# A delta-rule attention and a cosine feed-forward layer on one core: the order of 2143 tasks written anew

## The chip, the cores and the metric

The kernel runs on one core of a Trainium2 chip. The metric is device time in microseconds, from the first to the last instruction of the core and what lies around it; lower is better. The engines are TensorE (PE in the profile, with its weight loads as PEld), VectorE (DVE), ScalarE (ACT), GpSimd (POOL) and SyncE (SP), which here only issues DMAs.

## The reference

The first half is a recurrence over 768 steps with a 48 x 48 state for each of 4 x 8 heads, the second half a feed-forward layer with the activation h cos(h) on the 3072 x 384 result.

```python
k_n = k / (np.linalg.norm(k, axis=-1, keepdims=True) + 1e-06)
for t in range(S):                                   # S = 768, B = 4, H = 8, D = 48
    kt, vt, bt = (k_n[:, :, t], v[:, :, t], beta[:, :, t, None])
    y[:, :, t] = np.einsum('bhd,bhde->bhe', q[:, :, t], state)
    v_old = np.einsum('bhde,bhd->bhe', state, kt)
    state = state + bt[:, :, :, None] * np.einsum('bhd,bhe->bhde', kt, vt - v_old)
x = y.transpose(0, 2, 1, 3).reshape(3072, 384)
h = x @ w_in                                         # 384 x 2048
out = (h * np.cos(h)) @ w_out                        # 2048 x 384
```

## The kernel before

**Tasks.** The sequence is cut into 24 units of 32 steps; two units make a pair. The kernel first writes down 2143 tasks, each with a key, a Python function that issues its instructions on one engine, the tasks that it depends on, and the buffers that it makes and uses. Then `Order.run` (line 195) calls them one after the other in the order of `LINE` (line 79), a list of 2143 numbers, each the place of a task in the list of keys: 497 is `eye(7)`, 449 is `put(6)`, 739 is `hidden(0,0)`. At the end each engine's instructions are pinned to one another, so `LINE` fixes the order of every engine's queue and of SyncE's. A task that must wait holds up all that stands behind it on its engine. The costs and due times given to `add` are not used by `run`.

**Sides.** `OTHER` (line 49) holds the keys of tasks that go to their second engine: `x_sum` goes to GpSimd, or to VectorE if named in `OTHER`; `left` and `in_sums` go to VectorE, or to GpSimd if named; `fold` and `unfold` go to VectorE, or to ScalarE if named.

**Attention.** For each unit n, `k(n)`, `q(n)` and `v(n)` load keys, queries and values (from unit 8 on, `blocks` loads keys and queries once more, for a transpose on VectorE). `square`, `sum`, `norms` and `scale` form the norms of the keys; `turn` and `turn_out` transpose; `gram` multiplies keys with keys and queries, and `gram_keys` and `gram_queries` copy the result out of PSUM. A unit's triangular system is inverted next. In units 0 to 3 this is done on the spot: `fold`, `fold_in` and `fold_off` split the matrix, `rows` (TensorE) spreads its rows and `eliminate` works them off, on VectorE for groups 0 and 1 (units 0 and 1) and on GpSimd for group 2 (units 2 and 3, through `rows_copy` on ScalarE); then come `unfold`, `solve_half`, `half_out`, `between` and `between_out`. From unit 4 on a pair m is inverted on GpSimd: `gram_put` (L760) writes both matrices to DRAM, `gram_get(m)` (L769) reads them back into `gb`, `eye(m)` (L776, ScalarE) fills `z` with the identity, `inv(m,0)` to `inv(m,6)` (L791, L798) invert, `put(m)` (L802) writes `z` to DRAM, and `get(2m)` and `get(2m+1)` (L811) fetch it as the blocks that `solve` multiplies with. There is one `gb` and one `z`, so `eye(m+1)` waits until `put(m)`'s DMA has read `z`. Then follow `solve` (L891), `solve_out` (L901), `update` and `update_out` (the state, L914, L922), `within` (L931), `within_out`, `features` and `features_out` (the unit's columns of x). `state(n)` (L828) needs `update_out(n-1)`: the units are a chain.

**Feed-forward.** The weights come as 64-bit words and are narrowed on the chip: `weights(t)`, `split(t)`, `shift(t)` and `add(t)` on SyncE, ScalarE, VectorE and GpSimd. Pairs 0 and 1 compute h plainly (`hidden`, L971, 24 matrix products each), the other ten with twenty block products instead of 24: sums of parts of x (`x_sum`, L1064) and of w_in (`in_sums`, L1111) are multiplied in `layer(p,i)` (L1149) and put together in `layer_out` (L1161, L1163 on ScalarE, L1166 on VectorE). The activation is `turns` (L1012, ScalarE), `rest` (L1019, VectorE), `cos` (L1028, ScalarE) and `gate` (L1031, VectorE). The last product is plain in pair 0 (L1172) and Strassen's seven products from pair 1 on: `out(p,step,part)` (L1229), with `left` (L1245) forming sums of the activations, `right` (L1258) sums of w_out, `collect` (L1281, one in seven on ScalarE, L1268) adding the products up, and `store` (L1293) writing the output. PSUM holds three banks for h and two halves of one for the output.

The few lines that decide the order:

```python
line = [keys[int(i)] for i in self.LINE.split()]
for key in line:
    emit, deps, makes, uses = self.tasks[key]
    assert deps <= done, key
    emit()
```

Of the kernel before, what the change touches and what calls it, by code (L numbers as in the profile page):

```python
# [46 lines left out]
class Order:  # L47

    OTHER = {
        ('weigh', 0, 0), ('fold', 0), ('unfold', 0), ('weigh', 0, 1), ('fold', 1), ('unfold', 1),  # L50
        ('fold', 2), ('fold', 3), ('unfold', 2), ('unfold', 3), ('in_sums', 6), ('in_sums', 8),
        ('in_sums', 14), ('in_sums', 15), ('x_sum', 2, 'd'), ('x_sum', 2, 'n'), ('x_sum', 2, 'm'),
        ('x_sum', 2, 'e'), ('x_sum', 2, 'k'), ('x_sum', 2, 'g'), ('x_sum', 2, 'i'),
        ('x_sum', 2, 'l'), ('x_sum', 2, 'f'), ('x_sum', 2, 'h'), ('x_sum', 2, 'b0'),
        ('left', 2, 1, 0), ('left', 2, 2, 0), ('left', 2, 3, 1), ('x_sum', 3, 'd'),
        ('x_sum', 3, 'n'), ('x_sum', 3, 'm'), ('x_sum', 3, 'e'), ('x_sum', 3, 'k'),
        ('x_sum', 3, 'g'), ('x_sum', 3, 'i'), ('x_sum', 3, 'l'), ('x_sum', 3, 'h'),
        ('x_sum', 3, 'b0'), ('left', 3, 1, 0), ('left', 3, 4, 0), ('x_sum', 4, 'd'),
        ('x_sum', 4, 'n'), ('x_sum', 4, 'm'), ('x_sum', 4, 'e'), ('x_sum', 4, 'k'),
        ('x_sum', 4, 'l'), ('x_sum', 4, 'f'), ('x_sum', 4, 'h'), ('x_sum', 4, 'b0'),  # L60
        ('left', 4, 4, 0), ('left', 4, 3, 0), ('left', 4, 3, 1), ('x_sum', 5, 'd'),
        ('x_sum', 5, 'n'), ('x_sum', 5, 'k'), ('x_sum', 5, 'g'), ('x_sum', 5, 'b0'),
        ('left', 5, 1, 1), ('left', 5, 4, 0), ('left', 5, 3, 0), ('left', 5, 3, 1),
        ('x_sum', 6, 'd'), ('x_sum', 6, 'n'), ('x_sum', 6, 'k'), ('x_sum', 6, 'g'),
        ('left', 6, 1, 0), ('left', 6, 2, 0), ('left', 6, 2, 1), ('left', 6, 4, 1),
        ('left', 6, 3, 0), ('x_sum', 7, 'd'), ('x_sum', 7, 'n'), ('x_sum', 7, 'm'),
        ('x_sum', 7, 'l'), ('x_sum', 7, 'h'), ('x_sum', 7, 'b0'), ('left', 7, 1, 0),
        ('left', 7, 3, 0), ('x_sum', 8, 'd'), ('x_sum', 8, 'n'), ('x_sum', 8, 'm'),
        ('x_sum', 8, 'g'), ('x_sum', 8, 'l'), ('x_sum', 8, 'h'), ('x_sum', 8, 'b0'),
        ('x_sum', 9, 'd'), ('x_sum', 9, 'f'), ('left', 9, 1, 0), ('left', 9, 2, 0),  # L70
        ('left', 9, 1, 1), ('left', 9, 4, 0), ('left', 9, 4, 1), ('left', 9, 3, 0),
        ('left', 9, 3, 1), ('x_sum', 10, 'd'), ('x_sum', 10, 'n'), ('x_sum', 10, 'm'),
        ('x_sum', 10, 'g'), ('x_sum', 10, 'i'), ('x_sum', 10, 'l'), ('x_sum', 10, 'b0'),
        ('left', 10, 1, 0), ('left', 10, 2, 1), ('left', 10, 3, 0), ('x_sum', 11, 'd'),
        ('x_sum', 11, 'n'), ('x_sum', 11, 'f'), ('x_sum', 11, 'h'), ('left', 11, 1, 0),
        ('left', 11, 4, 0), ('left', 11, 4, 1), ('left', 11, 3, 0), ('left', 11, 3, 1),
# [1729 lines left out]
```

## Time and profile before

| | |
|---|---|
| time, median of 3 runs | 652.16 us (648.83 to 653.66) |
| span of the profiled execution | 654.2 us |
| TensorE busy | 619.1 us, 95%, 12306 matrix instructions |
| VectorE busy | 505.7 us, 77%, 948 instructions |
| ScalarE busy | 265.5 us, 41%, 469 instructions |
| GpSimd busy | 451.1 us, 69%, 788 instructions |
| chain that ended last | PE 72%, POOL 8%, DVE 7%, DMA 6%, issue 3% |

Busy times are of one execution under the profiler, whose span is its own time. A line of instructions gives the engine, the line of the code, the operation, what it wrote and read, and in brackets the idle time of the engine before it with what ended it. SPq is SyncE's queue, where the time is that of issuing DMAs.

### The profile page before, as it was taken

How to read it: one execution, taken by the hardware profiler on the slowest of the kernel's cores; microseconds unless marked ns; L12 is line 12 of the kernel's file. 1: busy time of each engine (PE TensorE's matmuls, PEld its weight loads, DVE VectorE, ACT ScalarE, POOL GpSimd, SP SyncE). 2: the span in 40 equal slices, each digit the busy share in tenths (PEclk: the TensorE clock that was granted, in tenths of full speed). 3: DMA queues.
4: the chain of work that ended last, by engine and by line, in shares of the span. 5: the costliest groups of instructions: out<-in, count | busy, mean ns of one | idle time of the engine just before them, and what ended most of it. 6: DMA issues, size and time to landing. Idle time of an engine off the chain costs nothing.

```text
span 654.2 us, 28227 instructions
## 1 busy us (share of the span) xinstructions
PE 619.1 (95%) x12306; PEld 579.8 (89%) x12306; DVE 505.7 (77%) x948; ACT 265.5 (41%) x469; POOL 451.1 (69%) x788
## 2 busy tenths in 40 slices
PE   5879799999999999998899999999999999999996
PEld 4778798976989999898799999999999999999996
DVE  7789798878999979776787877777777668667681
ACT  3545575731224523611542533622534523435340
POOL 3348989978988888686788986697787584143103
PEclk9979899999999999999799999999999999999999
DMA  7882573555444554434415434423400403000001
GB/s 157 192 217 72 130 217 82 118 107 75 90 68 67 115 73 71 95 67 81 77 29 93 67 62 77 90 40 62 85 7 13 105 4 60 13 2 25 2 13 36
DMA packets 202623, 49.99 MB, mean 76 GB/s; under 512 B 194244, under 2 KB 197460, under 8 KB 202500
## 3 DMA queue, kind: packets, MB, share of 16 engines
q1 hardware_dynamic: 201236, 47.81, 38.0%
q8 instruction: 96, 1.57, 1.0%
q10 hardware_dynamic: 1088, 0.20, 0.2%
q0 software_dynamic: 176, 0.18, 0.1%
q14 instruction: 27, 0.22, 0.1%
HBM read 38.19 MB, written 9.96 MB: 74 GB/s over the span
## 4 chain that ended last, share of the span: by engine, by line
PE 72%; POOL 8%; DVE 7%; DMA 6%; issue 3%; SPq 2%; ACT 2%; DVEq 0%; ACTq 0%; POOLq 0%
PE p_out L1229 23%; PE p_h L1149 23%; PE p_h L971 7%; PE p_out L1172 3%; DMA out_dram<-o 3%; PE p_kq L828 3%; PE p_u L891 2%; PE p_s L914 2%; POOL z L798 2%; POOL part L791 2%; PE p_kq L931 2%; PE p_g L619 2%; DVE turns L1019 1%; DMA qp<-in_q_dram 1%; PE p_z L950 1%
## 5 line engine op out<-in xcount | busy, mean ns | idle before, releaser
L791 POOL TENSOR_TENSOR part<-z,gb 128x126 f32<-128x126 f32 (+22 forms) x310 | 139.4, 450 | 56.2 <-DMA gb<-g_dr 15.7
L798 POOL TENSOR_TENSOR z<-z,part 128x126 f32<-128x126 f32 (+22 forms) x310 | 140.5, 453 | 24.4
L1229 PE MATMUL p_out<-w_out,g_ffn 128*128 128x192 f32 x672 | 122.5, 332 | 1.5 <-DVE o L1281 1.5
L1229 PEld LDWEIGHTS p_out<-w_out,g_ffn 128*128 128x128 f32 x672 | 109.0, 192 | 3.0 <-issue 1.1
L1028 ACT ACTIVATE turns<-turns,halfpi 128x512 f32<-128x512 f32 x96 | 68.7, 721 | 75.4 <-DVE turns L1019 74.8
L1229 PE MATMUL p_out<-w_sum,g_ffn 128*128 128x192 f32 x496 | 89.6, 329 | 1.8 <-DVE o L1281 1.8
L1245 POOL TENSOR_TENSOR g_ffn<-g_ffn 128x512 f32<-128x512 f32 x34 | 46.6, 1380 | 62.1 <-DVE g_ffn L1031 31.8
L1149 PE MATMUL p_h<-x_sum,w_in 128*128 128x128 f32 x640 | 84.8, 279 | 0.7 <-DVE g_ffn L1166 0.7
L1229 PEld LDWEIGHTS p_out<-w_sum,g_ffn 128*128 128x128 f32 x496 | 79.6, 191 | 2.9 <-DVE o L1281 2.2
L1149 PEld LDWEIGHTS p_h<-x_sum,w_in 128*128 128x128 f32 x640 | 78.7, 193 | 2.7 <-DVE g_ffn L1166 1.5
L1012 ACT ACTIVATE turns<-g_ffn,quarter_turn 128x512 int32<-128x512 f32 x70 | 50.0, 720 | 48.4 <-DVE g_ffn L1166 32.6
L1166 DVE TENSOR_TENSOR g_ffn<-g_ffn,p_h 128x512 f32<-128x512 f32 x80 | 54.2, 680 | 14.7 <-PE p_h L1149 12.1
L1019 DVE SCALAR_TENSOR_TENSOR turns<-g_ffn,turns 128x512 f32<-128x512 f32 x70 | 57.6, 831 | 8.6 <-ACT turns L1012 8.5
L1031 DVE TENSOR_TENSOR g_ffn<-turns,g_ffn 128x512 f32<-128x512 f32 x70 | 52.6, 758 | 12.7 <-ACT turns L1028 12.7
L1281 DVE SCALAR_TENSOR_TENSOR o<-p_out,o 128x192 f32<-128x192 f32 x74 | 25.1, 352 | 39.8 <-PE p_out L1229 29.7
L1149 PE MATMUL p_h<-x_sum,in_sum 128*128 128x128 f32 x400 | 54.2, 280 | 1.1 <-ACT p_h L1161 0.6
L971 PE MATMUL p_h<-x_ffn,w_in 128*128 128x128 f32 x384 | 50.4, 293 | 1.5 <-ACT row_copies L712 1.5
L1149 PEld LDWEIGHTS p_h<-x_sum,in_sum 128*128 128x128 f32 x400 | 49.2, 192 | 2.3 <-ACT p_h L1161 0.8
L971 PEld LDWEIGHTS p_h<-x_ffn,w_in 128*128 128x128 f32 x384 | 47.9, 206 | 2.5 <-ACT row_copies L712 1.6
L535 POOL TENSOR_TENSOR knrm<-ksum,halves 128x16 f32<-128x16 f32 (+1 forms) x14 | 37.0, 2646 | 15.7 <-DVE ksum L523 9.0
L1245 DVE TENSOR_TENSOR g_ffn<-g_ffn 128x512 f32<-128x512 f32 x54 | 42.5, 789 | 0.9 <-POOL part L791 0.3
L1149 PE MATMUL p_h<-x_ffn,w_in 128*128 128x128 f32 x320 | 42.8, 277 | 0.0
(144 smaller groups left out, 1041.5 us busy)
## 6 DMA issues: line engine op xcount, KB each, us to landing
gb<-g_dr SPq DMA_DIRECT2D x20, 256.0 KB
vp<-in_v_dram SPq DMA_DIRECT2D x96, 48.0 KB
in_sum<-in_moe_w_out_dram SPq DMA_DIRECT2D x12, 384.0 KB
out_dram<-o SPq DMA_DIRECT2D x23, 192.0 KB
in_sum<-in_moe_w_in_dram SPq DMA_DIRECT2D x8, 512.0 KB
kp<-in_k_dram SPq DMA_DIRECT2D x128, 24.0 KB
z_dr<-z SPq DMA_DIRECT2D x10, 256.0 KB
zt<-z_dr SPq DMA_DIRECT2D x80, 32.0 KB
```

The source lines that it names most:

```text
L535: nc.gpsimd.tensor_tensor(out=scales[m][2][:, part], in0=sums[m, part.start][:, 0:n], in1=halves[:, 0:n], op=ALU.pow,)
L791: nc.gpsimd.tensor_tensor(out=part, in0=z[:, 0:rows, j, None].to_broadcast(shape), in1=a[:, j, None, j + 1 :].to_broadcast(shape), op=ALU. ...
L798: nc.gpsimd.tensor_tensor(out=behind, in0=behind, in1=part, op=ALU.subtract)
L971: nc.tensor.matmul(p_h[:, i], w_in[:, t, (4 * k + i) * 128 : (4 * k + i + 1) * 128], xts[p][:, t, unit * 128 : (unit + 1) * 128], start=(i ...
L1012: nc.scalar.activation(turns[p, f], hidden_of(p, f), AF.Identity, bias=quarter_turn, scale=TURN)
L1019: nc.vector.scalar_tensor_tensor(out=r, in0=hidden_of(p, f), scalar=TURN, in1=t, op0=ALU.mult, op1=ALU.subtract,)
L1028: nc.scalar.activation(r, r, AF.Sin, bias=halfpi, scale=2.0 * math.pi)
L1031: nc.vector.tensor_tensor(out=place(p, f), in0=step_of(rests.pop((p, f)), f), in1=step_of(hidden_of(p, f), f), op=ALU.mult,)
L1149: nc.tensor.matmul(p_h[:, e], in_block(*w)[:, e], x_of(p, b), start=new and e == 0, stop=True, skip_group_check=True,)
L1166: nc.vector.tensor_tensor(out=part_of(p, to), in0=part_of(p, one), in1=part_of(p, two), op=op)
L1229: nc.tensor.matmul(p_o, left(p, part, a)[:, e % 4], right(e, b), start=(e == 0), stop=(e == FT // 2 - 1), skip_group_check=True,)
L1245: either(("left", p, x, s), nc.vector, nc.gpsimd).tensor_tensor(out=left(p, s, to), in0=left(p, s, one), in1=left(p, s, two), op=op)
```

## The change

The list `LINE` is replaced by another permutation of the same 2143 numbers, and `OTHER` by another set. Nothing else is touched: the tasks, their instructions, buffers and dependencies are the same. 31 `x_sum` go from VectorE to GpSimd and 19 the other way; 16 `left` go from GpSimd to VectorE and 15 the other way; four `in_sums` go from GpSimd to VectorE and one the other way; three `fold` and one `unfold` go from ScalarE to VectorE.

```diff
     OTHER = {
-        ('weigh', 0, 0), ('fold', 0), ('unfold', 0), ('weigh', 0, 1), ('fold', 1), ('unfold', 1),
-        ('fold', 2), ('fold', 3), ('unfold', 2), ('unfold', 3), ('in_sums', 6), ('in_sums', 8),
-        ('in_sums', 14), ('in_sums', 15), ('x_sum', 2, 'd'), ('x_sum', 2, 'n'), ('x_sum', 2, 'm'),
...
+        ('weigh', 0, 0), ('unfold', 0), ('weigh', 0, 1), ('fold', 1), ('unfold', 1),
+        ('unfold', 2), ('in_sums', 18), ('x_sum', 2, 'n'), ('x_sum', 2, 'm'), ('x_sum', 2, 'k'),
+        ('x_sum', 2, 'g'), ('x_sum', 2, 'i'), ('x_sum', 2, 'l'), ('x_sum', 2, 'f'),
...
     LINE = """
-2031 0 1 9 10 2 3 15 16 17 11 54 55 18 56 57 21 4 60 22 23 19 58 61 62 6 24 25 26 27 28 30 34 63 64
-29 93 92 101 65 66 32 102 31 2032 2035 2036 73 95 33 35 36 37 14 123 39 20 40 96 97 2037 2039 2038
...
+9 92 0 15 16 1 2 2031 3 2035 123 54 2039 21 93 17 4 60 55 11 6 22 7 95 18 10 56 57 19 96 23 5 61 62
+24 26 27 28 63 64 29 2032 2043 126 25 124 14 30 2033 2047 32 34 97 101 39 2034 65 31 127 2036 2040
...
```

In the names of the tasks, the stretches of the two orders that come up below (`-` before, `+` after), each a part of one queue:

```
ScalarE, around eye(7)
- layer_out(4,30) turns(4,(0,1,0)) eye(7) cos(4,(0,1,0)) turns(4,(1,0,0)) cos(4,(1,0,0))
  layer_out(5,5) layer_out(5,1) turns(4,(1,1,0)) square(8,0) turns(4,(1,0,1))
+ layer_out(4,30) features_out(11) turns(4,(0,1,1)) cos(4,(0,1,1)) turns(4,(1,0,0)) cos(4,(0,1,0))
  turns(4,(0,0,1)) cos(4,(1,0,0)) layer_out(5,5) layer_out(5,1) square(8,0) eye(7) turns(4,(1,0,1))
SyncE, around put(6)
- k(19) gram_put(14) gram_put(15) put(6) gram_get(7) get(12)
+ k(19) gram_put(14) gram_put(15) put(6) blocks(17,1) gram_get(7) get(12)
TensorE, ahead of solve(12)
- out(3,5,1) layer(5,15) out(3,6,0) solve(12)
+ layer(5,15) out(3,5,0) out(3,5,1) layer(5,4) layer(5,10) layer(5,1) out(3,6,0) solve(12)
SyncE, start
- weights(0) q(2) k(2) weights(1) v(0) k(3) weights(2) q(3) weights(3) q(4) weights(4)
+ k(2) weights(0) weights(1) k(3) weights(2) q(2) weights(3) q(3) v(0) weights(4) q(4)
TensorE, start
- gram(0) gram(1) rows(0,0) rows(0,2) turn(2) rows(0,1) rows(1,2) rows(0,3) state(0) turn(3)
+ gram(0) gram(1) rows(0,0) rows(0,1) rows(0,2) turn(2) state(0) rows(0,3) turn(3)
ScalarE, start
- square(0,0) square(0,1) turn_out(0) turn_out(1) fold(0) fold_off(0) fold(1) turn_out(2) split(0)
+ square(0,0) square(0,1) turn_out(0) square(1,0) turn_out(1) fold_off(0) split(0) square(1,1) fold(1)
VectorE, start
- scale(0,1) spread(0,0) spread(0,1) gram_keys(0) gram_queries(0) fold_in(0) gram_keys(1)
  gram_queries(1) begin_rows(0) fold_in(1) eliminate(0,0) eliminate(0,1) eliminate(0,2) eliminate(0,3)
  right(0) sum(1,0) shift(1) shift(0) shift(2) between_out(0)
+ scale(0,1) spread(0,0) sum(1,0) gram_keys(0) fold(0) fold_in(0) gram_keys(1) gram_queries(1)
  begin_rows(0) gram_queries(0) shift(0) eliminate(0,0) sum(1,1) eliminate(0,1) fold_in(1)
  eliminate(0,2) eliminate(0,3) right(0) scale(1,0) shift(3) scale(1,1) shift(2) between_out(0)
TensorE, from rows(1,3) on
- rows(1,3) gram(3) hidden(0,0) rows(2,0) rows(2,1) rows(2,2) solve_half(1) between(1) hidden(0,2)
  solve(1) rows(2,3) update(1) rows(2,4) within(1)
+ rows(1,3) rows(2,0) rows(2,1) hidden(0,0) solve_half(1) rows(2,2) between(1) rows(2,3) rows(2,4)
  solve(1) hidden(0,2) update(1) within(1)
SyncE, end
- store(10,1) store_left(11) store(10,0) store(11,1) store_right(11)
+ store(10,0) store(10,1) store_left(11) store(11,1) store_right(11)
```

More of the change, by code (lines that the diff above doesn't have):

```diff
@@ L49 @@
     OTHER = {
-        ('weigh', 0, 0), ('fold', 0), ('unfold', 0), ('weigh', 0, 1), ('fold', 1), ('unfold', 1),
-        ('fold', 2), ('fold', 3), ('unfold', 2), ('unfold', 3), ('in_sums', 6), ('in_sums', 8),
-        ('in_sums', 14), ('in_sums', 15), ('x_sum', 2, 'd'), ('x_sum', 2, 'n'), ('x_sum', 2, 'm'),
-        ('x_sum', 2, 'e'), ('x_sum', 2, 'k'), ('x_sum', 2, 'g'), ('x_sum', 2, 'i'),
-        ('x_sum', 2, 'l'), ('x_sum', 2, 'f'), ('x_sum', 2, 'h'), ('x_sum', 2, 'b0'),
-        ('left', 2, 1, 0), ('left', 2, 2, 0), ('left', 2, 3, 1), ('x_sum', 3, 'd'),
@@ L56 @@
[L56 to L73, printed above, removed]
@@ L74 @@
-        ('left', 10, 1, 0), ('left', 10, 2, 1), ('left', 10, 3, 0), ('x_sum', 11, 'd'),
-        ('x_sum', 11, 'n'), ('x_sum', 11, 'f'), ('x_sum', 11, 'h'), ('left', 11, 1, 0),
-        ('left', 11, 4, 0), ('left', 11, 4, 1), ('left', 11, 3, 0), ('left', 11, 3, 1),
+        ('weigh', 0, 0), ('unfold', 0), ('weigh', 0, 1), ('fold', 1), ('unfold', 1),
+        ('unfold', 2), ('in_sums', 18), ('x_sum', 2, 'n'), ('x_sum', 2, 'm'), ('x_sum', 2, 'k'),
+        ('x_sum', 2, 'g'), ('x_sum', 2, 'i'), ('x_sum', 2, 'l'), ('x_sum', 2, 'f'),
@@ new lines @@
+        ('left', 2, 1, 0), ('left', 2, 3, 1), ('x_sum', 3, 'i'), ('x_sum', 3, 'l'),
+        ('x_sum', 3, 'f'), ('x_sum', 3, 'h'), ('x_sum', 3, 'b0'), ('left', 3, 4, 0),
+        ('left', 3, 3, 1), ('x_sum', 4, 'd'), ('x_sum', 4, 'n'), ('x_sum', 4, 'm'),
+        ('x_sum', 4, 'e'), ('x_sum', 4, 'h'), ('left', 4, 1, 0), ('left', 4, 3, 1),
+        ('x_sum', 5, 'd'), ('x_sum', 5, 'n'), ('x_sum', 5, 'm'), ('x_sum', 5, 'e'),
+        ('x_sum', 5, 'i'), ('x_sum', 5, 'h'), ('left', 5, 4, 0), ('left', 5, 4, 1),
@@ new lines @@
+        ('left', 5, 3, 0), ('left', 5, 3, 1), ('x_sum', 6, 'd'), ('x_sum', 6, 'n'),
+        ('x_sum', 6, 'm'), ('x_sum', 6, 'k'), ('x_sum', 6, 'g'), ('x_sum', 6, 'i'),
+        ('x_sum', 6, 'l'), ('x_sum', 6, 'b0'), ('left', 6, 2, 0), ('left', 6, 2, 1),
+        ('left', 6, 4, 0), ('left', 6, 4, 1), ('x_sum', 7, 'd'), ('x_sum', 7, 'm'),
+        ('x_sum', 7, 'g'), ('x_sum', 7, 'l'), ('x_sum', 7, 'h'), ('x_sum', 7, 'b0'),
+        ('left', 7, 1, 1), ('left', 7, 3, 0), ('left', 7, 3, 1), ('x_sum', 8, 'f'),
@@ new lines @@
+        ('x_sum', 8, 'h'), ('left', 8, 1, 0), ('left', 8, 3, 0), ('left', 8, 3, 1),
+        ('x_sum', 9, 'n'), ('x_sum', 9, 'e'), ('x_sum', 9, 'i'), ('x_sum', 9, 'f'),
+        ('left', 9, 1, 0), ('left', 9, 4, 0), ('left', 9, 4, 1), ('left', 9, 3, 1),
+        ('x_sum', 10, 'd'), ('x_sum', 10, 'g'), ('x_sum', 10, 'f'), ('x_sum', 10, 'h'),
+        ('left', 10, 2, 0), ('left', 10, 4, 1), ('left', 10, 3, 0), ('left', 10, 3, 1),
+        ('x_sum', 11, 'd'), ('x_sum', 11, 'n'), ('x_sum', 11, 'm'), ('x_sum', 11, 'i'),
@@ L77 @@
+        ('x_sum', 11, 'l'), ('x_sum', 11, 'h'), ('left', 11, 1, 0), ('left', 11, 2, 0),
+        ('left', 11, 1, 1), ('left', 11, 2, 1), ('left', 11, 3, 0),
     }
     LINE = """
[98 rows of a table removed]
[97 rows of a table added]
 """
```

191 rows, old and new, of the table LINE are left out of this document.

## The prediction

> **What bounds the kernel now.** I read the page first: busy times, the forty slices, the granted clock.
>
> ```profile
> PE 619.1 (95%) x12306; PEld 579.8 (89%) x12306; DVE 505.7 (77%) x948; ACT 265.5 (41%) x469; POOL 451.1 (69%) x788
> ...
> PE   5879799999999999998899999999999999999996
> ...
> PEclk9979899999999999999799999999999999999999
> ```
>
> TensorE is busy in 95% of the span, so a new order can only remove its idle time, or the time in which its clock is halved. The second view is the table by stage (columns: window, its length, then busy time and instruction count of PE, weight loads, VectorE, ScalarE and GpSimd, granted clock, DMA share, GB/s):
>
> ```profile
> 0.00:50.00 50.00, 36.36 (x789) 32.26 (x790) 39.70 (x120) 23.42 (x47) 21.19 (x22) 0.88 0.82 188
> 50.00:100.00 50.00, 45.28 (x1241) 40.49 (x1241) 44.20 (x81) 30.08 (x63) 43.01 (x68) 0.95 0.54 138
> 100.00:160.00 60.00, 58.60 (x1219) 48.04 (x1219) 48.24 (x85) 26.93 (x49) 51.87 (x90) 1.00 0.49 96
> 160.00:300.00 140.00, 136.87 (x3150) 129.35 (x3149) 122.38 (x224) 49.53 (x85) 118.69 (x223) 1.00 0.48 81
> 300.00:320.00 20.00, 15.23 (x206) 14.54 (x206) 13.24 (x26) 6.25 (x10) 11.12 (x23) 0.83 0.54 90
> 320.00:440.00 120.00, 118.63 (x2495) 113.89 (x2478) 93.80 (x168) 48.84 (x84) 98.16 (x178) 1.00 0.40 66
> 440.00:600.00 160.00, 158.85 (x2933) 152.65 (x2912) 114.71 (x200) 64.03 (x108) 96.91 (x182) 1.00 0.19 38
> 600.00:654.30 54.30, 49.23 (x344) 48.58 (x342) 29.46 (x52) 16.44 (x27) 10.14 (x8) 0.99 0.06 17
> ```
>
> TensorE idles 18.4 us in the first 100 us, 4.8 us between 300 and 320, and under 3 us in all of 320 to 600. The gains can lie in the first two places only; after 320 a new order has almost nothing to win. The third view is the timeline around the one large hole, ScalarE, VectorE, SyncE's queue and TensorE in turn:
>
> ```profile
> 295.14 0.72 ACT L1012 ACTIVATE turns<-g_ffn,quarter_turn 128x512 int32<-128x512 f32 x1
> 309.44 0.62 ACT L776 COPY z<-consts 128x512 f32<-128x512 f32 x1 [13.58 <-DMA z_dr<-z]
> ...
> 306.68 0.36 DVE L1281 SCALAR_TENSOR_TENSOR o<-p_out,o 128x192 f32<-128x192 f32 x1 [0.46 <-PE p_out L1229]
> 311.33 0.69 DVE L1019 SCALAR_TENSOR_TENSOR turns<-g_ffn,turns 128x512 f32<-128x512 f32 x1 [4.29 <-ACT turns L1012]
> ...
> 301.38 3.66 SPq L760 DMA_DIRECT2D g_dr<-g  x6
> 305.16 0.54 SPq L802 DMA_DIRECT2D z_dr<-z  x1
> ...
> 313.61 1.51 PE L891 MATMUL p_u<-rhs,zt 32*32 32x48 f32 x64 [4.77 <-DVE g_ffn L1031]
> ```
>
> There is one z buffer. `eye(7)` (L776) may refill it only when `put(6)`'s DMA has read it. That DMA is issued at 305.16, behind two `gram_put` tasks on SyncE's queue, and lands at 309.4. ScalarE stands 13.6 us in front of it, VectorE then lacks the turns behind it (4.3 us), TensorE lacks VectorE (4.8 us). Then the clock is halved: start to start, `solve(12)` takes 1.44 us against the usual 0.77, half a product 2.72 against 1.30, a layer step 1.20 against 0.89, 2.4 us lost.
>
> **The change part by part.** To compare the orders I laid the durations of the rows end to end along every engine's queue, old and new, and asked for each handover how much work stands ahead of giver and taker.
>
> *Sides.* GpSimd gains twelve `x_sum` net (45 to 57) at 0.64 us and gives up one `left` at 1.38 and three `in_sums` at 1.68: +7.7 - 1.4 - 5.0 = +1.3 us. VectorE: -12 x 0.41 + 0.79 + 3 x 0.86, and from ScalarE three `fold` and one `unfold`, bounded by VectorE's `fold_in` (0.35) and ScalarE's `unfold` (0.69): about -0.5 to +0.2. These engines idle 203 and 149 us; the totals cost nothing. ScalarE sheds 1.9 us. TensorE's work is the same.
>
> VectorE's row with one operand in PSUM and that with both in SBUF:
>
> ```profile
> L1019 DVE SCALAR_TENSOR_TENSOR turns<-g_ffn,turns 128x512 f32<-128x512 f32 x70 | 57.6, 831 | 8.6 <-ACT turns L1012 8.5
> L1019 DVE SCALAR_TENSOR_TENSOR turns<-p_h,turns 128x512 f32<-128x512 f32 x26 | 17.5, 680 | 2.8 <-ACT turns L1012 2.8
> ```
>
> [...]
>
> *The hole at 309.* In the new ScalarE order seven tasks that stood behind `eye(7)` stand ahead of it: two `turns`, two `cos`, two `layer_out`, one `square`, 2 x 0.71 + 2 x 0.72 + 2 x 0.58 + 0.83 = 4.9 us. So VectorE gets its turns while the DMA is under way. On TensorE 2.7 us more work stands ahead of `solve(12)` (272.4 to 275.1). On SyncE `put(6)` still stands behind both `gram_put` tasks; `get(12)`, which `solve(12)` needs, now has a `blocks` task (four issues, 2.05 us) ahead of it, which the DMA's 4.2 us cover. If `get` still lands near 313.3, TensorE, there at 308.8 + 2.7 + 0.6, waits 1.2 us with an undisturbed clock. Gain 7.2 at best, 6.0 then, 3.6 if the clock halves all the same. I take -7.0.
>
> *Start.* Old: `eliminate(0,1)` waits 2.57 us for `rows(0,1)`, which stood behind `turn(2)` on TensorE; new: it stands ahead. But `k(2)` now leads SyncE's queue, and `square(1,0)` and `sum(1,0)`, which need it, stand ahead of `turn_out(1)` and `gram_keys(0)`. `k(1)`, issued until 5.86, was squared at 8.58; so `k(2)`, issued until about 9.9, lands about 12.6, and `gram_keys(0)` goes from 12.4 to about 13.7; `shift(0)` (1.1 us) and `sum(1,1)` (0.55) also go ahead. 2.6 - 1.3 - 1.7: nothing gained. Later: two `shift` and two `scale` (4.2 us) instead of one `sum` and three `shift` (5.8) before `between_out(0)`, which was 1.3 us late: -0.9. `solve(1)` no longer stands behind `hidden(0,2)` (2.9 us), which goes behind it instead, where `solve_out(1)` (1.0) is awaited anyhow: -0.6. `rows(2,0)` and `rows(2,1)` stand ahead of `hidden(0,0)`, so group 2's elimination on GpSimd starts up to 3 us sooner, and of the waits for its copies (0.59 + 0.74 + 1.55) I take 1.0 as gone. Together -2.5; ends: -6 (all of that, and 1.7 us of half clock at 72) and +3 (`k(2)` or `v(0)` late, with 1.3 + 1.7 us uncovered).
>
> *VectorE's lead.* Its work comes earlier against TensorE's: ahead of `update_out(5)` 127.4 us instead of 123.7, of `update_out(11)` 228.8 instead of 224.4, of `collect(7,3)` 384.3 instead of 376.1. If none of this fell into VectorE's idle time, TensorE would be held up to 3.9 us between 160 and 300 (at `out(1,3,0)`) and up to 6.9 between 440 and 600 (at `out(7,0,0)`). VectorE idles 17.6 and 45.3 us there. Ends 0 and +10.8; I take +1.0 for each stretch, nearer to nothing for that cover.
>
> *End.* The two stores of pair 10 change places; `collect` (L1281) waited for a store's landing until 643.6, which cost TensorE 0.34: -0.3.
>
> Sum against the profiled execution: 654.2 - 7.0 - 2.5 + 2.0 - 0.3 = 646.4. That execution lay 2.0 above the median, 652.16; against the median the forecast is **644.4 us**.
>
> **The rivals.** Each is set against the median.
>
> *VectorE eats the gain.* Hole gone (-6), no gain at the start, VectorE's lateness shows once in each stretch at half its bound or more (+6): **652**. For it: 22 of some 38 TensorE tasks between 160 and 200 would have under 0.3 us of slack, against 4. Against: its idle time.
>
> *Slower: VectorE never regains.* Each pair of units loses the 3 us anew, in pairs 2 to 4 and 7 to 9: 6 x 3 = 18, less 7 for the hole: 652.2 + 11 = **663**. It decides where VectorE's busy share in a stretch goes over about 0.95, so that lateness is carried on. For it: it is 0.96 between 160 and 180 already, and three `in_sums` come to it just before. Against: after 320 it is under 0.8.
>
> *More is won.* The start saves 5, and of the waits at 153.9, 181.6 and 403.4 (1.4, 1.6, 1.0) three go, beside the hole: 652.2 - 7.2 - 5 - 3 = **637**. For it: they all are VectorE's order. Against: VectorE's lead.
>
> [...]
>
> **How the numbers follow.** Forecast 0.42 (own range 639 to 651), VectorE eats the gain 0.24, slower 0.22, more is won 0.12. About 1%, 6.5 us, is what can be told from no change. Of the forecast 0.29 lies under 645.6 and 0.13 above; with the last rival, faster is 0.41; same 0.13 + 0.24 = 0.37; slower 0.22. The range, 635 to 661, leaves out the far part of the slow rival and little below.
>
> **What would show it.** Right: ScalarE's wait at L776 falls from 20.2 us in sum to under 9, no TensorE gap over 3 us after 100, no half clock after 100, TensorE's idle time to 100 us at 15 to 17 instead of 18.4. The VectorE step is wrong if TensorE's waits for L1281, L1166, L1245 or L901 between 160 and 600 sum to over 5 us. The forecast is wrong if another `eye` or `get` makes a hole as at 309, or if `hidden(0,0)` starts after 50 us instead of 47.0.

## The result and the profile after

The changed kernel takes 673.03 us at the median (669.73 to 675.67) against 652.91 for the kernel before on the same chip: 1.0301 times as long, 95% interval 1.0264 to 1.0338. The forecast was 644.4, the range 635 to 661. The profiled execution has a span of 668.0 us, against 654.2.

Busy times, TensorE's busy slices and its granted clock, from the page of the changed kernel:

```profile
PE 621.7 (93%) x12306; PEld 583.7 (87%) x12306; DVE 500.9 (75%) x945; ACT 265.7 (40%) x464; POOL 446.6 (67%) x796
...
PE   5779899999998998998999899998998999999997
...
PEclk9667999999999998999999999998999999999999
```

All engines do about as much as before; TensorE's share fell from 95 to 93%. The table by stage (same columns as before) says where:

```profile
0.00:50.00 50.00, 33.24 (x773) 29.00 (x773) 39.69 (x117) 21.23 (x41) 22.28 (x23) 0.75 0.76 177
50.00:100.00 50.00, 46.93 (x1191) 42.21 (x1192) 41.11 (x83) 32.08 (x65) 36.98 (x57) 0.91 0.54 140
160.00:300.00 140.00, 134.23 (x2962) 127.44 (x2961) 113.27 (x207) 50.77 (x87) 112.98 (x220) 0.98 0.45 73
300.00:320.00 20.00, 17.62 (x363) 17.09 (x363) 14.01 (x27) 6.10 (x10) 14.78 (x28) 1.00 0.54 91
320.00:440.00 120.00, 114.41 (x2516) 109.14 (x2515) 90.69 (x165) 47.77 (x82) 91.20 (x180) 1.00 0.40 68
440.00:600.00 160.00, 155.05 (x2898) 149.34 (x2897) 113.76 (x199) 62.28 (x105) 97.29 (x183) 0.99 0.21 38
```

The hole at 309 is gone (17.6 busy of 20, clock 1.00), as forecast. But TensorE now idles 5.8 us between 160 and 300 instead of 3.1, 5.6 between 320 and 440 instead of 1.4, and 5.0 between 440 and 600 instead of 1.2, where nothing was to happen, and the clock in the first 50 us fell from 0.88 to 0.75. TensorE's waits between 160 and 600 (us in sum, times, longest):

```profile
PE p_g L614 <- issue: 10.1, 5, 2.5
PE p_h L1144 <- issue: 3.9, 2, 2.6
PE p_kq L823 <- issue: 1.6, 2, 1.3
PE p_u L886 <- DMA zt<-z_dr: 1.0, 1, 1.0
```

"issue" means that the profile shows nothing that the engine waited for: no semaphore, no DMA, no bank. The same stretch of the kernel before has one such line:

```profile
PE p_h L1149 <- issue: 0.4, 1, 0.4
```

(Line numbers are five lower in the changed file: L1224 was L1229.) One of them on TensorE's timeline:

```profile
210.98 0.80 PE L614 MATMUL p_g<-kq_t 48*32 48x64 f32 x60
...
211.63 1.36 PE L823 MATMUL p_kq<-st,kq_t 48*32 48x48 f32 x127
212.82 0.27 PE L614 MATMUL p_g<-kq_t 48*32 48x64 f32 x2
215.60 1.14 PE L614 MATMUL p_g<-kq_t 48*32 48x64 f32 x62 [2.52 <-issue]
216.66 2.07 PE L1144 MATMUL p_h<-x_sum,in_sum 128*128 128x128 f32 x8
```

TensorE stops two matmuls into `gram(11)`, although `gram_queries(10)` had given the bank back at 212.63. The tasks `gram(10)`, `state(8)`, `gram(11)` stand one behind the other here; in the old order two products and two layer steps stood between the grams. A gram is 64 matrix instructions and as many weight loads, 128 in 0.79 us; a state 256 in 1.31 us; a layer step is 16 in 0.89 us. So the three tasks are 512 instructions in under 3 us. In the trace's DMA records there is a queue called "instruction", q8, with 96 packets of 16384 bytes, one for every 256 of TensorE's 24,612 instructions. One packet begins at 213.17, inside the gap, and lands at 214.09; TensorE goes on 1.5 us later. The nine largest gaps after 100 us all end a streak of this kind. TensorE idles 17.0 us in them (1.3 to 2.6 each); with what is slowed around them, the tasks that they interrupt take 19.6 us more than usual. In all nine TensorE goes on 1.2 to 1.6 us after such a packet has landed. Half products and layer steps at half the clock, right behind four of them, take another 4.3 us.

### The profile page after: what moved, and what is told of

Read it like the earlier page. It is cut to its first block, busy times and chain, and to the rows that moved or that the text cites. A ratio compares the mean times of both kernels' runs of the same rounds, so it can differ in the third digit from the quotient of the medians.

```text
span 668.0 us, 28208 instructions
## 1 busy us (share of the span) xinstructions
PE 621.7 (93%) x12306; PEld 583.7 (87%) x12306; DVE 500.9 (75%) x945; ACT 265.7 (40%) x464; POOL 446.6 (67%) x796
## 4 chain that ended last, share of the span: by engine, by line
PE 69%; POOL 13%; DMA 6%; issue 6%; SPq 3%; DVE 2%; ACT 1%; POOLq 0%; DVEq 0%; ACTq 0%
PE p_out L1224 22%; PE p_h L1144 20%; PE p_h L966 5%; POOL part L786 5%; POOL z L793 5%; PE p_kq L823 4%; PE p_g L614 3%; PE p_out L1167 3%; PE p_s L909 2%; PE p_kq L926 2%; PE p_u L886 2%; PE p_r L696 2%; DMA gb<-g_dr 2%; PE p_o L1224 2%; POOL g_ffn L1240 1%
## 5 line engine op out<-in xcount | busy, mean ns | idle before, releaser
L786 POOL TENSOR_TENSOR part<-z,gb 128x126 f32<-128x126 f32 (+22 forms) x310 | 136.5, 440 | 55.2 <-DMA gb<-g_dr 15.1
L793 POOL TENSOR_TENSOR z<-z,part 128x126 f32<-128x126 f32 (+22 forms) x310 | 142.0, 458 | 24.3
L1224 PE MATMUL p_out<-w_out,g_ffn 128*128 128x192 f32 x672 | 123.6, 332 | 1.1 <-DVE o L1276 1.1
L1224 PEld LDWEIGHTS p_out<-w_out,g_ffn 128*128 128x128 f32 x672 | 109.6, 193 | 2.4 <-issue 1.4
L1224 PE MATMUL p_out<-w_sum,g_ffn 128*128 128x192 f32 x496 | 89.3, 329 | 1.0 <-POOL z L793 1.0
L1144 PE MATMUL p_h<-x_sum,w_in 128*128 128x128 f32 x640 | 83.3, 277 | 2.8 <-issue 2.6
L1224 PEld LDWEIGHTS p_out<-w_sum,g_ffn 128*128 128x128 f32 x496 | 80.3, 192 | 1.6 <-POOL z L793 1.1
L1240 POOL TENSOR_TENSOR g_ffn<-g_ffn 128x512 f32<-128x512 f32 x33 | 45.1, 1377 | 37.9 <-PE p_out L1224 29.9
L1026 DVE TENSOR_TENSOR g_ffn<-turns,g_ffn 128x512 f32<-128x512 f32 x70 | 56.8, 816 | 11.8 <-ACT turns L1023 11.6
L1014 DVE SCALAR_TENSOR_TENSOR turns<-g_ffn,turns 128x512 f32<-128x512 f32 x70 | 53.8, 774 | 12.6 <-ACT turns L1007 12.5
L1144 PE MATMUL p_h<-x_sum,in_sum 128*128 128x128 f32 x400 | 55.6, 285 | 1.3 <-issue 1.3
L1144 PEld LDWEIGHTS p_h<-x_sum,in_sum 128*128 128x128 f32 x400 | 51.1, 198 | 4.5 <-issue 3.9
L966 PE MATMUL p_h<-x_ffn,w_in 128*128 128x128 f32 x384 | 49.3, 289 | 0.5 <-issue 0.5
L1276 DVE SCALAR_TENSOR_TENSOR o<-p_out,o 128x192 f32<-128x192 f32 x74 | 25.2, 353 | 32.5 <-PE p_out L1224 32.3
L1144 PE MATMUL p_h<-x_ffn,w_in 128*128 128x128 f32 x320 | 42.4, 277 | 0.0
```

Of the source, the lines that this page charges most:

```text
L786: nc.gpsimd.tensor_tensor(out=part, in0=z[:, 0:rows, j, None].to_broadcast(shape), in1=a[:, j, None, j + 1 :].to_broadcast(shape), op=ALU. ...
L793: nc.gpsimd.tensor_tensor(out=behind, in0=behind, in1=part, op=ALU.subtract)
L966: nc.tensor.matmul(p_h[:, i], w_in[:, t, (4 * k + i) * 128 : (4 * k + i + 1) * 128], xts[p][:, t, unit * 128 : (unit + 1) * 128], start=(i ...
L1014: nc.vector.scalar_tensor_tensor(out=r, in0=hidden_of(p, f), scalar=TURN, in1=t, op0=ALU.mult, op1=ALU.subtract,)
L1026: nc.vector.tensor_tensor(out=place(p, f), in0=step_of(rests.pop((p, f)), f), in1=step_of(hidden_of(p, f), f), op=ALU.mult,)
L1144: nc.tensor.matmul(p_h[:, e], in_block(*w)[:, e], x_of(p, b), start=new and e == 0, stop=True, skip_group_check=True,)
```

## The experiments

**Theory A.** TensorE runs out of instructions where short ones are packed. **Theory B**, the rival, and near to the slow rival of the prediction: VectorE and GpSimd are late, by their order or their sides, and the gaps are where TensorE meets that.

**The disputed cost by itself.** Behind the last matmul of the kernel before, work is added that waits for nothing.

```diff
+    p_x = bank("kq", [128, 2, 512], "p_x")
...
+    short(2)     # 2 x 32 matmuls of a gram's shape
+    long(48)     # 128 x 128 x 128
+    short(2)
+    long(48)
+    short(16)
```

> The kernel before with a piece of TensorE work added behind its last matmul, whose result nothing uses: 2 blocks of the short matmuls of a gram (256 instructions with the weight loads), 48 long ones (128 by 128 by 128), 2 short blocks again, 48 long ones, then 16 short blocks in a row (2048 instructions). No bank or semaphore stands between them. Theory A (a packet of 256 instructions every 3.4 to 3.8 us, and a store of some 450): no gap in the two pieces of 2 blocks, 0.8 us each block; in the piece of 16 the first 450 instructions at that pace, then gaps, 256 instructions per 3.4 to 3.8 us, 24 to 27 us for the piece. Theory B (the gaps were waits for banks or for VectorE): 16 x 0.79 = 12.6 us, no gaps.

TensorE's timeline at the end of that kernel:

```profile
655.31 1.48 PE L1776 MATMUL p_x<-consts 48*32 48x64 f32 x128
656.72 10.98 PE L1784 MATMUL p_x<-consts 128*128 128x128 f32 x96
667.64 2.11 PE L1776 MATMUL p_x<-consts 48*32 48x64 f32 x193
671.54 1.47 PE L1776 MATMUL p_x<-consts 48*32 48x64 f32 x128 [1.80 <-issue]
675.29 2.04 PE L1776 MATMUL p_x<-consts 48*32 48x64 f32 x128 [2.28 <-issue]
```

256 instructions (128 matrix instructions and their loads) go through without a gap. The long streak stops after 193 + 193 = 386, and then 256 come every 3.5 to 4.0 us, with a gap in front of each: 26.7 us for what 16 x 0.74 = 11.8 us would do. The granted clock is 1.00 up to 674 us and 0.50 from then on, so the first gap came at the full clock. Each time TensorE goes on 1.3 to 1.5 us after a packet of the instruction queue has landed, and none came between 661.0 and 669.2 us. From 661.0 the long matmuls used up 115 instructions; with the 386 of the streak an estimated 500 lay ready then, about two packets. Theory A holds, here without any other engine. The mechanism as this run shows it: the streak used up 386 instructions that lay ready, and from then on got 256 per 3.5 to 4.0 us.

**The packing put into the kernel before**, on TensorE's queue alone, for five pairs of grams; one of them:

```diff
-gram(12) layer(3,17) layer(3,5) gram(13) out(2,5,0) out(2,5,1) layer(4,18) layer(4,15) out(2,6,0) state(10)
+layer(3,17) layer(3,5) gram(12) state(10) gram(13) out(2,5,0) out(2,5,1) layer(4,18) layer(4,15) out(2,6,0)
```

> The kernel before, with five pairs of grams (6 and 7, 8 and 9, 10 and 11, 12 and 13, 14 and 15) drawn together with the state task beside them, as the changed kernel has them, by moving tasks of TensorE's queue alone by up to six places. Theory A (instructions run out): each of the five streaks ends in a gap of 1.5 to 3 us that no semaphore ends; 652.9 rises by 7 to 15, to 660 to 668. Theory B (VectorE's order and sides): TensorE does the same work with the old VectorE order, so 651 to 655.

666.2 us, 1.0248 times the kernel before (1.0217 to 1.0279): 15.6 us more, with every other queue and every side as it was. TensorE's waits at the grams after 100 us, and the streak above on its timeline:

```profile
PE p_g L618 <- issue: 6.1, 4, 2.4
...
261.95 0.83 PE L618 MATMUL p_g<-kq_t 48*32 48x64 f32 x63
265.15 0.31 PE L618 MATMUL p_g<-kq_t 48*32 48x64 f32 x1 [2.37 <-issue]
```

Four of the five streaks have a gap that ends with issue, two of them as long as theory A had it (2.1 and 2.4 us; the others 1.2 and 0.4). The grams drawn together also wait for VectorE, 4.9 us in sum: `gram(7)` 1.3, `gram(11)` 2.7, `gram(15)` 0.9. And the clock is halved for 3.4 us behind four of the five. So of the 15.6 us, 6.1 are gaps for instructions, and the rest comes with the packing in other ways. Theory B cannot make this loss, since VectorE's and GpSimd's queues and sides are the old ones.

**The streaks parted in the changed kernel.** First only the nine `state` tasks were moved:

```diff
-out(1,6,0) layer(2,5) gram(10) state(8) gram(11) layer(3,18) out(1,6,1) layer(3,15) layer(3,1)
+out(1,6,0) layer(2,5) gram(10) gram(11) layer(3,18) out(1,6,1) layer(3,15) state(8) layer(3,1)
```

> The changed kernel, with nine state tasks (4, 6, 8, 10, 12, 14, 15, 18, 20) moved alone: each three or four places later on TensorE's queue (the first, five places earlier), so that long products and layer steps stand between it and the two grams it stood with. Every other queue and every side stays. Theory A (TensorE runs out of instructions: its instruction queue brings them in packets of 256, and gram, state, gram in a row are 512 of the shortest ones): the nine gaps of 1.5 to 3.1 us behind these streaks go, 19.6 us in sum, with some of the 4.3 us that the half clock costs behind four of them: 673.0 falls to 649 to 655, and the trace shows no gap over 1 us that ends with issue after 100 us. Theory B (VectorE's new order and sides are late, and the gaps are where TensorE happens to meet that): the time stays within 3 us of 673, the gaps move to the next tasks.

669.4 us, 1.0284 (1.0240 to 1.0328): no difference from the changed kernel's 1.0301 that can be told, far from theory A's 649 to 655 and just outside the 3 us of theory B. The gaps that ended with issue are gone but for one of 1.3 us at 108, and in their place TensorE's waits after 100 us are led by

```profile
PE p_g L614 <- DVE tt L737: 8.2, 8, 1.4
```

Both grams of a pair write one bank; the second must wait until VectorE has read the first. The state between them had covered that. So eight grams now wait 0.9 us or more. Theory A explains the gaps, but not the 20 us that were expected of their removal.

Then long tasks were set between the two grams as well:

```diff
-out(1,6,0) layer(2,5) gram(10) gram(11) layer(3,18) out(1,6,1) layer(3,15) state(8)
+gram(10) out(1,6,0) layer(2,5) gram(11) layer(3,18) out(1,6,1) layer(3,15) state(8)
```

> The changed kernel as in the run with the nine state tasks moved, and besides with two long tasks (products, layer steps or one hidden) between the two grams of each of the eight pairs, again on TensorE's queue alone. There the gaps that ended with issue were gone, but gram(2m+1) then stood 0.83 us for VectorE's gram_queries(2m), which reads the one bank that both grams write, eight times, 6.7 us in sum. Theory A (the changed order loses its time to its streaks of short matmuls, through instructions where they are packed and through the bank where they are not): those 6.7 us go too, 669.4 falls to 655 to 662. Theory C (TensorE runs only as far ahead as VectorE lets it, and what it wins at the grams it loses at out_out and the sums, as the new gaps of 1.3 to 1.7 us at 175, 309 and 323 us suggest): 666 to 670, with more such gaps.

665.6 us, 1.0244 (1.0204 to 1.0283), just under the range of theory C and 3.6 us above that of theory A. The bank's waits are down to 1.1 us after 100; the gain over the changed kernel is 0.57% with an uncertainty of about as much, some 4 us. Behind the 24 us of gaps and half clock other waits now show: a sum that is late before `layer(2,4)` (1.9 us), `out(3,4,0)` (2.6), the solve at 320 (1.5). The chain that ended last, in this kernel:

```profile
PE 39%; POOL 34%; DMA 7%; issue 7%; DVE 5%; SPq 5%; ACT 2%; POOLq 0%; DVEq 0%; ACTq 0%
```

Before it was PE 72%, POOL 8%, and in the changed kernel itself PE 69%, POOL 13%. With the streaks parted a third of the chain is GpSimd, 27% its inverses. This share does not go with the time, though: two runs below have POOL at 25% with a ratio of 1.0074 and at 7% with 1.0280.

**The sides alone.** The old order with the new `OTHER`, and the new order with the old one.

```diff
-    OTHER = {...}   # of the kernel before
+    OTHER = {...}   # of the changed kernel; LINE stays
```

> The kernel before with its order, and the table of sides of the changed kernel: the sums that change between VectorE and GpSimd change, nothing moves. Theory A (instructions run out; sides cost nothing): within 3 us of 652.9. Theory B (the sides make VectorE or GpSimd late): over 658, with TensorE waiting for x_sum, left or collect tasks.

739.9 us, 1.1385. VectorE and TensorE on the timeline at the largest gap:

```profile
255.23 0.29 DVE L1059 TENSOR_TENSOR x_sum<-x_sum 128x128 f32<-128x128 f32 x1 [18.54 <-POOL x_sum L1059]
...
255.89 1.44 PE L1144 MATMUL p_h<-x_sum,w_in 128*128 128x128 f32 x5 [14.57 <-POOL x_sum L1059]
```

A sum given to GpSimd stands behind the rest of an inverse in its queue, VectorE's next sum waits 18.5 us for it, and TensorE 14.6. That is theory B's case, over 658 with waits for sums, though no size near this was expected.

> The changed kernel's order with the table of sides of the kernel before: the counterpart of the run with the new sides in the old order, which took 739.9. Theory D (order and sides are one plan: a sum that changes its engine alone comes to stand behind an inverse on GpSimd's queue, and VectorE and TensorE wait for it): over 690. Rival (the new sides are themselves bad): below 673.

683.8 us, 1.0509 (1.0467 to 1.0551): between the two expectations, 2.0% above the changed kernel. The new sides are better than the old ones for the new order, and much worse for the old order; order and sides are one plan.

**The hole at 309 alone.**

```diff
-turns(4,(0,1,0)) eye(7) cos(4,(0,1,0)) turns(4,(1,0,0)) cos(4,(1,0,0)) layer_out(5,5) layer_out(5,1) turns(4,(1,1,0))
+turns(4,(0,1,0)) cos(4,(0,1,0)) turns(4,(1,0,0)) cos(4,(1,0,0)) layer_out(5,5) layer_out(5,1) turns(4,(1,1,0)) eye(7)
```

> The kernel before, with eye(7) alone moved on ScalarE's queue, behind two turns, a cos and two layer_out tasks that it held up. The prediction's term for the hole at 309 (-7.0, with ends -3.6 and -7.2): 644 to 649, and TensorE's gap of 4.8 us before solve(12) falls under 1.5. Rival (the hole only moves: the inverse that follows eye(7) or the get behind it is late by as much): 650 to 653, with a gap of 3 us or more at the next solve.

650.6 us against 650.6, ratio 1.0003 (0.9977 to 1.0029): the time as the rival had it, though the wait before `solve(12)` fell to 1.5 us:

```profile
PE p_u L890 <- DMA zt<-z_dr: 1.5, 1, 1.5
```

> The kernel before once more, unchanged, for a second profile. The first had a span of 654.2, 2.7 above the longest of the 17 spans shown since, and a gap of 4.8 us before solve(12). If the hole at 309 belongs to the order, it is here again, 4 to 5 us long, and the span is 644 to 652 all the same. If it belongs to that one execution (a late DMA of put(6)), the gap is under 2 us.

The second execution of the kernel before, with a span of 651.3, lies between the two expectations:

```profile
PE p_u L890 <- DVE tt L741: 3.2, 1, 3.2
```

The kernel with the short streak above has the old order up to its last matmul, and there TensorE's wait before `solve(12)` and ScalarE's for the z buffer are

```profile
PE p_u L891 <- DMA zt<-z_dr: 1.0, 1, 1.0
...
ACT z L776 <- DMA z_dr<-z: 11.2, 2, 9.8
```

So a wait there belongs to the order, but its size does not: 4.8 us in the first profile, 3.2 here, 1.5 in the spliced kernel below that keeps the old order up to 322 us, and 1.0 with the short streak. The 1.5 us after the move of `eye(7)` lie within that spread, so they cannot be put down to the move. The first profile, whose span of 654.2 lies above all others of that kernel (641.7 to 653.6), had it at its largest. That it is small in most executions fits the equal medians, but most were not profiled.

**Other causes of what is left.** With the streaks parted some 15 us remain.

> The same kernel with its grams and states apart, and with the first 320 tasks (the first 101 us) in the order and on the sides of the kernel before; the rest follows in the new order. Theory A: the start of the changed kernel costs 3 to 5 us by 100 us (hidden(0,0) at 55.2 against 47.0, the clock granted 0.75 against 0.88 in the first 50 us), so the time is 3 to 5 below the run with the grams and states apart alone. Rival (the start's loss is made up later, since VectorE or the inverses decide what follows): within 1.5 us of it.

670.4 us, 1.0302. The old start is 4.8 us worse, not better: behind the seam TensorE waits 2.4 us before `between(3)` and 1.6 before `update(3)` (104 and 115 us), with 3.4 us at half the clock between them. The run says nothing about the start.

SyncE's queue, on top of the parted streaks:

```diff
-k(17) blocks(16,0) v(14) v(15) k(18) blocks(16,1) store(2,0) k(19) gram_put(14) gram_put(15) put(6)
+store(2,0) k(17) blocks(16,0) v(14) v(15) k(18) gram_put(14) blocks(16,1) gram_put(15) k(19) put(6)
```

> The changed kernel with its grams and states apart, and besides, on SyncE's queue alone, stores, puts and gets ahead of the bulk loads (k, v, blocks) that they stood behind although their data were there: store(2,0), ready at 265, was issued at 303; put(6), ready at 307, at 312.7. Theory E (SyncE's new order makes VectorE wait for the o tiles and the inverses late): the gaps of 2.6 us before out(3,4,0) and 1.5 before solve(12) go, 4 to 6 us in all, 665.6 falls to 660 to 662. Rival (GpSimd and VectorE decide): within 1.5 us.

664.1 us, 1.0206 (1.0180 to 1.0232), about as the rival had it. The gap before `out(3,4,0)` went, but the wait before `solve(12)` grew from 1.5 to

```profile
PE p_u L886 <- DMA zt<-z_dr: 3.6, 1, 3.6
```

since inverse 6 ends at 308 as before. To that kernel the sums were given back to VectorE (`x_sum` of layers 2 to 5, then of all):

```diff
+        ('x_sum', 2, 'd'), ...   # 21 more in OTHER, then 57
```

> The changed kernel with grams and states apart and stores and puts ahead of the loads, and besides with the 21 sums (x_sum) of layers 2 to 5 that it gives to GpSimd on VectorE; their places in the order stay. Theory F (GpSimd is full: from 86 to 307 us its queue has 208 us of work and 17 of short waits, against 204 and 8 in the kernel before, so inverse 6 ends at 308 instead of 299, and TensorE stands 3.8 us at solve(12)): inverse 6 ends 6 to 10 us earlier, the gap at solve(12) goes under 1.5, 664.1 falls to 656 to 660. Theory G (VectorE is what TensorE lacks, as the gap of 1.9 us before layer(2,4) for a sum on VectorE says): 0.3 us more for each sum on VectorE between 100 and 320, 664 or more.

> The same with all 57 sums of layers 2 to 11 that the changed kernel gives to GpSimd on VectorE. Theory F: GpSimd has its inverses early enough to the end, 654 to 660. Theory G: VectorE, 80% busy to 560 us as it is, takes 17 us more work, and the time rises above 666.

664.5 (1.0218) and 667.5 (1.0280). Theory F falls: GpSimd has less to do, inverse 4 ends 4 us earlier, but its `put` then waits behind loads on SyncE's queue, and inverse 6 still ends at 308 to 311. The times are those of theory G, though 21 more sums on VectorE cost nothing that can be told, and all 57 some 0.7%.

> The kernel with grams and states apart and the 21 sums of layers 2 to 5 on VectorE, and besides put(m) and gram_get(m+1) ahead of the bulk loads on SyncE's queue, and the VectorE tasks that read the odd grams right behind them. Theory H (the chain of the inverses on GpSimd sets the end: in every profile so far the end comes 109 to 115 us after inverse 11, which ended at 536 to 545 in the old order and 551 to 555 in the new; one inverse waits for put, eye and gram_get of the one before it, 93 to 106 us in sum over nine turns, and sums in the queue make the inverses 4 to 16 us longer in sum): inverses as short as in the run with the sums on VectorE (364 us) and turns as short as with the stores first (94) give 87 + 364 + 94 = 545 for inverse 11 and 657 to 659 for the kernel. Rival (the chain only follows TensorE and VectorE, which are late for reasons of their own): inverse 11 ends at 551 or later again, 663 or more.

685.6 us, 1.0528: inverse 11 ended at 566, later than in any other kernel with the streaks parted. With loads behind puts, and reads of the odd grams ahead of the sums, VectorE's `collect` holds TensorE 14 us. The rival is right by its numbers. Theory H is not borne out, and the run does not refute it either, since it brought waits of its own.

**Where the rest arises.** Old and new plan were joined at a seam where they differ by six tasks, each with its own sides.

> Two plans spliced: the first 745 tasks (to 223 us) in the order and on the sides of the kernel before, the rest in the order of the changed kernel with its grams and states apart, on the new sides. At the seam the two differ by six tasks. By the loss of TensorE in the profiles (time gone less work done), the loosened new order stands 4.7 us behind the old one at 223 us, 12 at 322, 13 at 420 and 15.4 at the end. If the loss is made where it shows: 652 + 10.7, so 660 to 664. Rival (it is made before 223 and only shows later): within 3 us of the kernel before.

> The same with the first 1100 tasks (to 322 us) from the kernel before. If the loss is made where it shows: 3.4 us more than the kernel before, 653 to 657. Rival (the last part of the new order costs as much as the middle): 659 or more.

> The counterpart: the first 1100 tasks in the loosened new order and on the new sides, the rest as the kernel before has it. If the loss is made where it shows: 12 us more than the kernel before, 661 to 666. Rival: 656 or less.

661.9 (1.0182, 1.0143 to 1.0222), 654.4 (1.0074, 1.0040 to 1.0107) and 664.7 (1.0235, 1.0192 to 1.0277), all three where the loss shows in TensorE's trace. By differences of the ratios, out of 2.4% for the parted kernel, 0.6% arise before 223 us, 1.1% between 223 and 322, and 0.7% after that, each with an uncertainty of about half a per cent. (The two halves at 322 add up to 3.1%, so a seam costs something itself.)

**The kernel before, loosened** by the same rule: `eye(7)` later, and `hidden(0,8)` between `state(2)` and `gram(4)`.

```diff
-features(1) state(2) gram(4) rows(2,7) hidden(0,8) gram(5)
+features(1) state(2) hidden(0,8) gram(4) rows(2,7) gram(5)
```

> The kernel before with two moves: eye(7) behind the five ScalarE tasks that it held up, and hidden(0,8) ahead of gram(4) instead of behind it, so that a long task parts state(2) and gram(4), where TensorE ran out of instructions at 71 us (1.6 us, and 1.6 more while the clock was halved behind it). Theory A: 2 to 4 us below the kernel before, 647 to 649, with no gap at 71. Rival (the start's chain of rows decides, and gram(4) is only later): within 1.5 us.

652.7 us, 1.0018 (0.9989 to 1.0047). The half clock behind the gap at 71 us is gone, but the gap is not: TensorE stood 1.6 us before `hidden(0,8)` and now stands 1.4, at 68 us. Both profiles name ScalarE's copy of the rows (`rows_copy`) as what ended it, and `hidden(0,8)` starts within 0.1 us of the copy's end. So that gap was no want of instructions, and the rival has it right. No version here beats the kernel before.

## Why the prediction was wrong

**The step that failed** is a half sentence of the part on the sides, "TensorE's work is the same", and with it the way of the sum: durations laid end to end along each queue, as if a task's length did not depend on its neighbours. The same 12306 matrix instructions cost 15.6 us more when five pairs of grams were packed in the old order, and nothing else; 6.1 us of it were gaps for instructions. In the changed kernel such gaps came to 17.0 us after 100. No term and no rival had it, though the new order of TensorE's queue was there to be read, and 128 instructions in 0.79 us could be counted.

**In the new order, though, this is not the whole loss.** Parting the streaks gave back some 4 us, and with SyncE's stores first 6, of 20. That fits an overlap, TensorE standing still for instructions while VectorE and GpSimd caught up, but no run shows it by itself. What the remaining 2% come from is located, nearly a half of it between 223 and 322 us, but not settled. Taking away one wait at a time (bank, stores, sums on GpSimd) moved TensorE's gap to the next; inverse 11 ends at 551 to 555 us in the changed order and at 537 to 545 in the old one. In the old order with five streaks packed it ends at 552 as well, and inverse 6 at 309 instead of 300, although GpSimd's queue and sides are untouched there: TensorE's queue alone can make the inverses as late as that. Whether they lead or follow once the streaks are parted is open.

**The hole, -7.0.** The waits were read rightly in the first profile, but the step took them for a property of the old order. ScalarE's wait for the z buffer was 20.2 us there, and in the changed kernel

```profile
ACT z L771 <- DMA z_dr<-z: 10.9, 2, 8.2
```

(under 9 was expected), and TensorE waited 1.0 us before `solve(12)`; 1.2 was expected. But the old order shows 11.2 and 1.0 in the run with the short streak, so the change need not have made this difference. Taken alone the move is worth 0 within 2 us. The step took the largest of four sizes for the usual one, and -7.0 where its own working gave 6.0 for a wait of 1.2.

**The start, -2.5.** Not borne out. `hidden(0,0)` began at 55.2 us, past the 50 that was to refute the forecast; TensorE idled 19.8 us in the first 100, not 15 to 17. The old order idled 18.4, 20.2 and 19.1 in its three profiles (the last with the short streak), and in 100 us TensorE had issued 2028, 1961 and 1962 matrix instructions there, 1962 in the changed kernel. So nothing was won by 100 us, and a loss is not shown either.

**VectorE's lead, +2.0.** By the test that was set (waits for VectorE between 160 and 600 over 5 us) the term looks right: under 1 us. The test was blind, because the gaps for instructions hid those waits. With the gaps parted, waits for `collect` (L1276) on VectorE alone came to 4.8 us after 100 (3.3 in the kernel before), and the remaining loss of some 15 us is above the term's upper end, +10.8; how much of it is this term is not shown.

**The sides, 0.** Only true together with the order; alone they cost 89 us. A total over a queue says nothing about what a moved task stands behind. Why L1019 took 831 ns with both operands in SBUF and 680 with one in PSUM (774 and 685 in the changed kernel) no run shows; the sum has no term for it.

**The clock.** The prediction had the wait before `solve(12)` at 1.2 us "with an undisturbed clock". There it was 1.0 us, and the clock from 320 to 440 was 1.00. The rival "more is won" likewise set three waits of 1.4, 1.6 and 1.0 us down as 3 us. That a wait of this length costs no more than itself was the author's assumption. Three stretches of the changed kernel: busy, the gap behind `gram(7)`, and what follows; the column behind the counts is the granted clock.

```profile
126.40:128.70 2.30, 2.25 (x216) 2.10 (x216) 1.41 (x4) 1.64 (x4) 1.83 (x7) 1.00 0.65 81
128.70:130.30 1.60, 0.01 (x3) 0.01 (x2) 0.55 (x1) 0.72 (x1) 1.29 (x6) 1.00 0.00 0
130.30:133.70 3.40, 3.40 (x53) 3.23 (x53) 2.48 (x5) 0.00 (x0) 2.64 (x3) 0.50 0.66 108
```

A gap of 1.6 us was enough for 3.4 us at half the clock; behind a gap of 2.6 us at 382 the clock stayed at 1.00. The prediction had named no half clock after 100 as a sign of being right; there were four stretches of 3.4 us. Four of the nine gaps were followed by one, five were not, and their length does not tell which. So the assumption failed, and the prediction's own trace spoke against it: its part on the start counts 1.7 us of half clock at 72, behind a gap of 1.6.

**The rivals.** The nearest in time was "VectorE never regains", 663, with a chance of 0.22. Its mechanism, three us lost anew in each pair of units where VectorE is over 0.95 busy, was not what the trace of the changed kernel showed: VectorE's busy share is at most 0.92 in the 20-us windows from 160 on. That its number came nearest is luck. The range ended 12 us below the result.

## What to carry to other kernels

Count instructions, not only microseconds, along each stretch of TensorE's queue: where some 400 short ones follow one another in less time than instructions took to come here (256 in 3.5 to 4.0 us), put long matmuls between them, and leave them between two tasks that share a bank. Read an order and the sides of its tasks as one plan, and ask of every task that changes its engine what it will stand behind. Before a hole in one profile goes into a sum, see whether a second execution has it in the same size.

## What the runs showed of the hardware that was not expected

TensorE ran dry of instructions after a streak of 386 short ones that waited for nothing, and from then on got 256 per 3.5 to 4.0 us, 14 to 16 ns each, although the same instructions issue at 6 ns at the full clock (256 in 1.48 us) and 8 at half of it (256 in 2.04). In the profile such a gap has no releaser and reads as "issue"; in seven of seven here, and in nine of nine in the changed kernel, TensorE went on 1.2 to 1.6 us after a 16384-byte packet of the instruction queue had landed.
